# All paired groups of batches 2 and 3 through seven products that build on each other in PSUM

## The chip, the core and the metric

One core of a Trainium2 chip runs the whole program. The metric is the device time of one execution in microseconds (us), the median of some runs. The engines that matter here are TensorE (PE in the rows, its weight loads PEld), VectorE (DVE), ScalarE (ACT), GpSimd (POOL) and the queue of SyncE (SP), from which nearly all transfers are issued. TensorE's results go to eight banks of PSUM, which TensorE, VectorE and ScalarE reach.

## The reference

Capped attention, then two multi-layer parts with residuals, on 4 batches of 448 tokens and 768 columns:

```python
scores = cap * tanh(q @ k.T / sqrt(64) / cap)           # 12 heads of 64
attn = exp(scores - max) / (sum + 1e-9) @ v             # -> x: (4, 448, 768)
xn = (x - mean) / sqrt(var + 1e-6) * g_ln
x = x + relu(xn @ w_ch1) @ w_ch2                        # 768 -> 3072 -> 768
h = relu(x.T @ w_tok1) @ w_tok2                         # tokens: 448 -> 256 -> 448
u = x + h.T
y = u + relu(u @ w2_ch1) @ w2_ch2                       # 768 -> 1536 -> 768
```

## The kernel before

Activations lie transposed: `X[b][e]` is a block of 128 columns of batch `b` by 448 tokens, six blocks a batch. Every number that enters a product is kept as two halves, a rounded high one and the rest (`split`: ScalarE or VectorE copies the high half at L180 or L182, VectorE subtracts for the low half at L176), and a product takes three passes (`PASSES`), so it is three matmuls of 128x128 by 448 for each pair of blocks.

The channel layers are worked off in groups of 4 hidden blocks (512 hidden columns): 6 groups of the first MLP, 3 of the second. `mlp` runs a group directly, for one batch or two (first layer L926, second layer L899); a batch takes 144 matmuls a group, two take 288. For batches 2 and 3 most groups go another way: `strassen` treats the two batches and the halves of a weight block as a 2x2 problem and makes seven products where eight are direct, 252 matmuls (L713). For this it needs sums of quarter blocks of weights (`a11`, `a12`, `a21`, `a22` give `s1` to `s4`, in `sums`) and sums of the activations (`X1` to `X4`, in `sides`; `b11`, `b21` are batch 2's halves in `BIG[0]`, `b12`, `b22` batch 3's in `BIG[1]`). `first_quads` makes the hidden blocks of a group (two quads, `q` = 0, 1; each product nine matmuls), then sums of them (`H1` to `H4`, L640), and `second_quads` the outputs (each product three times, `r` = 0 to 2, six matmuls).

Before, each product has a bank of its own from a ring of eight; the sums of products are made outside PSUM: ScalarE copies a product (`out_copy`, L704), VectorE adds others to it (`plus`, L701) or adds two SBUF tiles (`both`, L640). `sums` makes weight sums in a chain: `start` loads a quarter from DRAM, `more` lets a transfer issued by GpSimd add another quarter onto it (L676), `negate` is ScalarE (L682), then `split`.

The weights come as 64-bit words that `piece` decodes on ScalarE and VectorE; the decoded whole and its halves are stored to DRAM (L340, L369), from where later uses load them (L353, and L733 and L797 for paired groups). This is done while batches 0 and 1 go through `mlp`. Groups 0 and 6 are lone for batches 2 and 3 (`N1 = 1`, `N2 = 1`): batch 2 runs group 0 after its norm, batch 3 runs it woven into the token mixing of batch 2 (`tokens`: transposes L960, first layer L984, second L1006), batch 2 runs group 6 woven into the mixing of batch 3, and batch 3 runs it after that.

The order is not that of the code. `Program.emit` collects all steps with keys (`prog.key`, a due time in the planner's us, less an `early`), and always takes the engine that can go first and on it the ready step with the smallest key, by its own table of costs (`FIXED`, `RATE`, `LATER`). The constants ahead of the program set the keys. On every engine and queue the steps are then worked off strictly in that order, so a step that waits holds up what stands behind it. Names with `late_` (`late_qk`, `late_vs`, `late_x0` and so on) are tiles that take over the space of attention's tiles; `late_bank` are the four banks that attention's scores had. `split0` to `split2` and `late_whole` are eight half tiles (`part_ring`) that hold weights for products.

## Time and profile before

| | us |
|---|---|
| median of 3 runs | 1364.21 (1359.86 to 1368.12) |
| the profiled execution | 1362.73 |
| its span, first to last instruction | 1361.0 |
| TensorE busy in it | 1317.1 (97%) |
| VectorE busy | 1160.7 (85%) |
| ScalarE busy | 766.7 (56%) |
| GpSimd busy | 236.6 (17%) |

Attention and the norms of batches 0 and 1 take the first 180 us; until about 780 us batches 0 and 1 go through their MLPs and mixings while attention of batches 2 and 3 runs beside them; the paired groups of the first MLP stand at 838 to 1112 us, the mixings of batches 2 and 3 at 1112 to 1244, the last two paired groups behind. A row of the profile that names two tiles, as in "bank<-big,split", writes the first from the others; buffer numbers are left out.

### The profile page before, as it was taken

To read this page: it belongs to the slowest core of one execution; us is meant where nothing else is said; L and a number is where in the kernel's file an instruction comes from. 1 tells how busy PE (TensorE), PEld (TensorE's weight loads), DVE (VectorE), ACT (ScalarE), POOL (GpSimd) and SP (SyncE) were. 2 spreads that over 40 slices of the span, in tenths; PEclk is the share of its full clock that TensorE was granted. 3 is DMA by queue.
4 is the path that set the end of the run, shared out by engine and by line. 5 is a ranking of instruction groups with operands and counts; after the bars stand their busy time and mean duration, and the time that the engine had idled before them with its cause. 6 is when DMAs were issued, how large, how long until landed. Compare 5 with 4: busy or idle time off the path is not lost. (4 is left out here: it accounts for less than half of the span.)

```text
span 1361.0 us, 18258 instructions
## 1 busy us (share of the span) xinstructions
PE 1317.1 (97%) x6234; PEld 1128.5 (83%) x6234; DVE 1160.7 (85%) x1999; ACT 766.7 (56%) x1227; POOL 236.6 (17%) x196
## 2 busy tenths in 40 slices
PE   8899999999999999999999999899999999999997
PEld 4334589999999899988899989788988889999786
DVE  5989799999999999999999874878888884476698
ACT  8996667675766756866765322634535442223442
POOL 2420000110101001200000030333323320011221
PEclk9999999999999999999999999999999999999899
DMA  7885357777777868466777587687787884357685
GB/s 279 307 276 194 119 185 250 276 256 284 247 253 263 281 236 279 151 222 224 246 249 246 199 258 246 133 189 168 172 188 166 199 212 143 116 170 184 133 196 129
DMA packets 163021, 290.12 MB, mean 213 GB/s; under 512 B 12016, under 2 KB 105840, under 8 KB 162928
## 3 DMA queue, kind: packets, MB, share of 16 engines
q1 hardware_dynamic: 131888, 266.64, 57.9%
q0 software_dynamic: 30464, 22.03, 11.9%
q8 instruction: 49, 0.80, 0.3%
q10 hardware_dynamic: 576, 0.29, 0.1%
q14 instruction: 44, 0.36, 0.1%
HBM read 203.39 MB, written 85.52 MB: 212 GB/s over the span
## 5 line engine op out<-in xcount | busy, mean ns | idle before, releaser
L899 PE MATMUL bank<-h,split 128*128 128x448 f32 x1452 | 312.4, 368 | 4.0 <-DMA split<-kept 1.8
L926 PE MATMUL bank<-big,split 128*128 128x448 f32 x1404 | 299.2, 368 | 0.5 <-DVE split L176 0.5
L899 PEld LDWEIGHTS bank<-h,split 128*128 128x128 f32 x1452 | 271.4, 188 | 29.2 <-issue 3.6
L926 PEld LDWEIGHTS bank<-big,split 128*128 128x128 f32 x1404 | 262.6, 188 | 25.2 <-issue 1.6
L176 POOL TENSOR_TENSOR ks<-qk,ks 64x512 fp32r<-64x512 f32 x24 | 34.6, 1444 | 497.1 <-ACT ks L419 488.3
L903 DVE TENSOR_TENSOR x<-x,bank 128x448 f32<-128x448 f32 x121 | 73.8, 610 | 24.3 <-PE bank L899 23.6
L180 ACT ACTIVATE split<-whole 128x512 fp32r<-128x512 f32 (+1 forms) x70 | 50.4, 721 | 60.5 <-PE bank L899 24.5
L931 ACT ACTIVATE h<-bank 128x448 fp32r<-128x448 f32 x78 | 42.1, 540 | 64.5 <-PE bank L926 64.3
L333 ACT ACTIVATE whole<-raw 128x512 f32<-128x512 f32 (+2 forms) x94 | 70.7, 752 | 12.5 <-DMA raw<-in_w 6.8
L336 DVE SCALAR_TENSOR_TENSOR whole<-raw,whole 128x512 int32<-128x512 int32 (+2 forms) x94 | 74.1, 788 | 0.1
L337 DVE CUSTOM_DVE_ANT_0 whole<-raw,whole 128x1024 uint16<-128x1024 uint16 (+2 forms) x84 | 71.3, 849 | 0.1
L334 ACT ACTIVATE raw<-raw 128x512 int32<-128x512 uint32 (+2 forms) x94 | 71.2, 758 | 0.1
L176 DVE TENSOR_TENSOR split<-whole,split 128x512 fp32r<-128x512 f32 (+1 forms) x80 | 64.9, 812 | 0.8 <-ACT split L180 0.6
L446 DVE TRANSPOSE_TENSOR_REDUCE m<-x 128x28 f32<-128x896 f32 x48 | 52.9, 1105 | 12.3 <-ACT x L442 11.9
L441 ACT ACTIVATE own<-sc,tsc 128x896 f32<-128x896 f32 x48 | 48.2, 1004 | 15.2 <-DVE x L502 7.9
L713 PE MATMUL bank<-big,split 128*128 128x448 f32 x222 | 52.7, 375 | 2.3 <-ACT split L180 2.2
L932 DVE SCALAR_TENSOR_TENSOR h<-bank,h 128x448 fp32r<-128x448 f32 x78 | 47.7, 611 | 8.1 <-ACT h L931 7.9
L335 DVE TENSOR_SCALAR whole<-whole 128x512 int32<-128x512 int32 (+2 forms) x94 | 52.3, 557 | 1.9 <-ACT whole L333 1.8
L446 DVE TRANSPOSE_TENSOR_REDUCE m<-own 128x28 f32<-128x896 f32 x48 | 52.7, 1097 | 0.9 <-ACT own L442 0.9
L493 DVE TRANSPOSE_TENSOR_REDUCE n<-own 128x28 f32<-128x896 f32 x48 | 52.5, 1097 | 0.0
L442 ACT ACTIVATE own<-own,cap_t 128x896 f32<-128x896 f32 x48 | 50.0, 1042 | 0.6
L438 PE MATMUL sc<-qs,ks 128*128 128x448 f32 x192 | 48.1, 371 | 1.9 <-ACT own L441 1.4
(426 smaller groups left out, 2803.1 us busy)
## 6 DMA issues: line engine op xcount, KB each, us to landing
split<-kept SPq DMA_DIRECT2D x94, 384.0 KB, 4.4
raw<-in_w SPq DMA_DIRECT2D x36, 768.0 KB, 5.4
kept<-split SPq DMA_DIRECT2D x36, 768.0 KB, 4.2
raw<-in_w SPq DMA_DIRECT2D x54, 512.0 KB, 3.8
split<-kept SPq DMA_DIRECT2D x42, 512.0 KB, 3.9
keeps<-split SPq DMA_DIRECT2D x42, 512.0 KB, 3.8
qk<-in_qkv SPq DMA_DIRECT2D x33, 480.0 KB, 4.3
whole<-whole SPq DMA_DIRECT2D x28, 384.0 KB, 2.8
```

What stands on the lines that cost most here:

```text
L176: eng.tensor_tensor(out, whole, high.bitcast(F32), op=ALU.subtract)
L333: add("act", m * 1.1, lambda: act(f.bitcast(F32), hi.bitcast(F32), AF.Copy, scale=2.0 ** -112), [r], [w])
L334: add("act", m * 1.1, lambda: act(lo, lo.bitcast(U32), AF.Copy, scale=2.0 ** -29), (), [r])
L335: add("dve+", m // 2, lambda: dve.tensor_scalar(f, f, 3, None, op0=ALU.logical_shift_left), (), [w])
L336: add("dve+", m, lambda: dve.scalar_tensor_tensor(f, hi, -(1 << 31), f, op0=ALU.bitwise_and, op1=ALU.bitwise_or), [r], [w])
L337: add("pool+" if ahead else "dve+", m, lambda e: engine_of[e].tensor_tensor(f, f, lo, op=ALU.add), [r], [w])
L446: add("dve", 2 * S, lambda half=half, e=e: dve.tensor_reduce(m.at[:, half].rearrange("p c j -> p (c j)"), e.rearrange("p c (j i) -> p (c j ...
L493: add("dve", 2 * S, lambda half=half, e=e: dve.tensor_reduce(n.at[:, half].rearrange("p c j -> p (c j)"), e.rearrange("p c (j i) -> p (c j ...
L713: mm(bank.at[:, :S], w(wi), x.at[:, xi], start=(i, n) == (0, 0), stop=(i, n) == (len(parts) - 1, 2))
L899: mm(py.at[:, :S], w[:, wi, i * P:(i + 1) * P], h[i].at[:, hi], start=(i, n) == (0, 0), stop=(i, n) == (G - 1, 2))
L903: add("dve", S, lambda x=x, py=py: dve.tensor_tensor(x.at, x.at, py.at[:, :S], op=ALU.add), [py], [x], early=EVACUATE)
L926: mm(ph.at[:, :S], w[:, wi, cc * P:(cc + 1) * P], src[cc].at[:, xi], start=(cc, n) == (0, 0), stop=(cc, n) == (NCC - 1, 2))
```

## The change

All nine groups of batches 2 and 3 are paired (`N1 = 0`, `N2 = 0`), and the mixings of the two batches are woven with each other (`tokens(2)` with `tokens(3)`). In a quad the product `a11*b11` stays in its bank: ScalarE copies it, and `s2*X2`, then `s1*X1`, then `s4*b22` are added onto it in the same bank by matmuls that don't start a new sum; `s3*X3` and `a22*X4` share another bank. `second_quads` does the same in three banks each, and VectorE adds each stage to `X`. Banks are handed out from a list (`spare`). Weight sums are made by four loads and four VectorE additions of 384 columns (`narrow`). `sides` takes the norm's results or `X` as they are where it can, and goes through its kinds one after another. In `tokens`, the second layer takes all three blocks with the first hidden block, then all three with the second. The wholes of second-layer weights are stored in another layout. All constants that set keys and some of the planner's costs are new.

The diff, cut to its core:

```diff
-URGENT, SCORES, PREPARE, LOAD = 1000.0, 19.31, 4.58, 24.58
+URGENT, SCORES, PREPARE, LOAD = 1000.0, 14.37295, 3.25093, 26.17876
...
-N0, N1, N30, N20, N2 = 1, 1, 0, 1, 1
...
+N0, N1, N30, N20, N2 = 1, 0, 0, 1, 0
...
+T_ATT2, PACE2, T_ATT3, PACE3 = 200.92224, 35.97238, 678.45284, 26.41417
...
-QUAD_LEAD, SUM_LEAD, SIDES_LATER, SIDES_PACE, X_LATER = 16.0, 24.0, 20.0, 4.0, 4.0
+QUAD_LEAD, SUM_LEAD, SIDES_LATER, SIDES_PACE, HIDDEN_LATER, FIRST = 3.35595, 16.17507, -13.10765, 1.12559, -1.8455, 0.95664
...
-            add("dma", m, lambda: nc.sync.dma_start(out=whole.at, in_=g), [w], [whole])
+            rows = g if m == C else g.rearrange("p (a d) -> p a d", a=G)
+            add("dma", m, lambda: nc.sync.dma_start(out=whole.at, in_=rows), [w], [whole])
...
-                    of_group[grp] = dp.tile([P, NCC, 2, cols], F32, name=f"keeps{grp}"), dp.tile([P, NCC, cols], F32, name=f"wholes{grp}")
+                    of_group[grp] = dp.tile([P, NCC, 2, cols], F32, name=f"keeps{grp}"), dp.tile([P, G, NCC, P], F32, name=f"wholes{grp}")
...
+    def sides(later, x2, x3, between=None):
+
+        t, t0 = [next(tmps) for _ in range(3)], prog.key
+        more = ring([next(tmps), next(tmps)])
+        for kind in range(4):
+            for c in range(3):
+                prog.key = t0 + later + (3 * kind + c) * SIDES_PACE
+                b12, b22, to = x3[c], x3[3 + c], t[c]
+                if kind == 0:
+                    b11 = x2[c] if x2 else to
+                    if not x2:
+                        join(b11, BIG[0][c], S)
+                    both(to, b12, b11, ALU.subtract, S)
+                elif kind == 1:
+                    both(to, to, b22, ALU.subtract, S)
+                elif kind == 2:
+                    to = next(more)
+                    both(to, b22, b12, ALU.subtract, S)
+                else:
+                    to = next(more)
+                    b21 = x2[3 + c] if x2 else to
+                    if not x2:
+                        join(b21, BIG[0][3 + c], S)
+                    both(to, b21, t[c], ALU.add, S)
+                split((X1, X2, X3, X4)[kind][c], to, S)
+            if kind == 2 and between:
+                between()
...
-    def sums(chunks, a11, a12, a21, a22, s1, s2, s3, s4):
...
-        def start(f, a):
-            at, boxes = a
...
-        def more(f, a):
-            at, boxes = a
-            add("pool", CC, lambda: nc.gpsimd.dma_start(out=shaped(f, at), in_=at, accum_op=ALU.add), boxes, [f], lag=4.0)
...
-        def negate(f):
-            add("act", CC, lambda: act(f.at, f.at, AF.Copy, scale=-1.0), (), [f])
...
-        split(s1, fa, CC)
-        negate(fa)
-        more(fa, a11)
-        split(s2, fa, CC)
-        more(fa, a12)
+    def sums(f11, f12, f21, f22, a11, a12, a21, a22, s1, s2, s3, s4):
+
+        def narrow(to, a, b, op):
+            add("dve+", CC, lambda: dve.tensor_tensor(to.at[:, :CC], a.at[:, :CC], b.at[:, :CC], op=op), [a, b], [to])
+
+        for f, (at, boxes) in ((f21, a21), (f22, a22), (f11, a11), (f12, a12)):
+            add("dma", CC, lambda f=f, at=at: nc.sync.dma_start(out=f.at[:, :CC], in_=at), boxes, [f])
+        narrow(f22, f21, f22, ALU.add)
+        narrow(f21, f11, f21, ALU.subtract)
+        narrow(f11, f11, f22, ALU.subtract)
+        split(s2, f11, CC)
+        split(s3, f21, CC)
+        narrow(f12, f12, f11, ALU.add)
...
-        split(s3, fb, CC)
+        split(s1, f22, CC)
         yield
-        split(s4, fa, CC)
+        split(s4, f12, CC)
...
+    def take():
+        return spare.pop(0)
+
+    def product(bank, parts, n_parts, first):
...
-                    mm(bank.at[:, :S], w(wi), x.at[:, xi], start=(i, n) == (0, 0), stop=(i, n) == (len(parts) - 1, 2))
+                    mm(bank.at[:, :S], w(wi), x.at[:, xi], start=first and (i, n) == (0, 0), stop=(i, n) == (len(parts) - 1, 2), skip_group_check=not first)
...
+    def quad(g, q):
...
+        a11, a12 = direct(row, 0), direct(row, CC)
+        c11 = next(tmps)
+        pa, pd = take(), take()
+        times(pa, a11, b11, first=True)
+        out_copy(c11, pa)
+        times(pd, a12, b21, first=True)
+        plus(c11, pd, c11)
+        spare.append(pd)
+        rectify(c11)
+        split(H11[q], c11, S)
+        yield
+        s2, s3, s1 = (next(part_ring) for _ in range(3))
+        a22, s4 = direct(row2, CC), next(part_ring)
+        prog.key -= SUM_LEAD
+        for _ in sums(*(next(wfs) for _ in range(4)), block(row, 0), block(row, CC), block(row2, 0), block(row2, CC), s1, s2, s3, s4):
+            pass
+        prog.key += SUM_LEAD
+        c21, c22, c12 = (next(tmps) for _ in range(3))
+        pc = take()
+        times(pa, s2, X2)
+        out_copy(c21, pa)
+        times(pc, s3, X3, first=True)
+        out_copy(c22, pc)
+        yield
+        times(pa, s1, X1)
+        plus(c22, pa, c22)
+        rectify(c22)
+        times(pc, a22, X4)
+        plus(c21, pc, c21)
+        spare.append(pc)
+        rectify(c21)
+        split(H21[q], c21, S)
+        split(H22[q], c22, S)
+        yield
+        times(pa, s4, b22)
+        rectify(c12, pa)
+        spare.append(pa)
+        prog.key += HIDDEN_LATER
+        both(c11, c12, c11, ALU.subtract, S)
+        both(c12, c22, c12, ALU.subtract, S)
+        both(c22, c11, c22, ALU.subtract, S)
+        both(c21, c21, c22, ALU.add, S)
+        split(H2[q], c22, S)
+        split(H3[q], c12, S)
+        split(H1[q], c11, S)
+        split(H4[q], c21, S)
+        prog.key -= HIDDEN_LATER
+        yield
...
+        def onto(b, e, bank):
+            plus(X[b][e], bank, X[b][e])
+
+        pa = [take() for _ in range(3)]
         for r in range(3):
-            p = times("a11", r, H11)
-            out_copy(t[r], p)
-            plus(X[2][r], p, X[2][r])
+            onto(2, r, times(pa, "a11", r, H11, first=True))
             yield
         further(QUAD_LEAD)
+        pd = [take() for _ in range(3)]
         for r in range(3):
-            p = times("a12", r, H21)
-            plus(X[2][r], p, X[2][r])
+            onto(2, r, times(pd, "a12", r, H21, first=True))
             final(2, r)
             yield
...
+        spare.extend(pd)
...
         for r in range(3):
-            plus(t[r], times("s2", r, H2), t[r])
-            both(w[r], w[r], t[r], ALU.add, S)
-            both(X[3][r], X[3][r], w[r], ALU.add, S, -X_LATER)
-            both(X[3][3 + r], X[3][3 + r], w[r], ALU.add, S, -X_LATER)
+            onto(2, 3 + r, times(pa, "s2", r, H2))
+            yield
+        further(QUAD_LEAD)
+        pc = [take() for _ in range(3)]
+        for r in range(3):
+            onto(3, 3 + r, times(pc, "s3", r, H3, first=True))
             yield
         for r in range(3):
-            p = times("s3", r, H3)
-            plus(X[3][3 + r], p, X[3][3 + r])
+            onto(3, 3 + r, times(pa, "s1", r, H1))
             final(3, 3 + r)
-            plus(t[r], p, t[r])
-            both(X[2][3 + r], X[2][3 + r], t[r], ALU.add, S, -X_LATER)
             yield
         for r in range(3):
-            plus(X[3][r], times("s4", r, H22), X[3][r])
+            onto(2, 3 + r, times(pc, "a22", r, H4))
+            final(2, 3 + r)
+            yield
+        spare.extend(pc)
+        for r in range(3):
+            onto(3, r, times(pa, "s4", r, H22))
             final(3, r)
             yield
-        for r in range(3):
-            plus(X[2][3 + r], times("a22", r, H4), X[2][3 + r])
-            final(2, 3 + r)
-            yield
+        spare.extend(pa)
...
         def second(half, hT):
-            for e in range(3 * half, 3 * half + 3):
-                pu, xb, g = next(main_banks), X[b][e], u[e]
-
-                def product(e=e, pu=pu):
-                    a = (e % 3) * P
-                    for j in range(2):
+            banks = {}
+            for j in range(2):
+                for e in range(3 * half, 3 * half + 3):
+                    if j == 0:
+                        banks[e] = next(main_banks)
+                    pu, xb, g = banks[e], X[b][e], u[e]
+
+                    def product(e=e, pu=pu, j=j):
...
+                    pe(3 * S, product, [hT[j], T2[j]], [pu])
+                    if j == 1:
...
+                    yield
...
-        relay()
-        sides(SIDES_LATER)
+        sides(SIDES_LATER, None, centred, relay())
...
+        spare += [next(main_banks) for _ in range(8)]
         weave(strassen(groups((2, 3), n1, NG1 - n1)))
+        main_banks = ring(list(spare))
...
-        weave(tokens(2, HIDDEN[2]), mlp(groups((3,), N30, n1 - N30)), ahead=TOKENS_AHEAD)
-        weave(tokens(3, HIDDEN[2]), mlp(groups((2,), NG1, n2)), ahead=TOKENS_AHEAD)
-        sides(SIDES_LATER)
+        if N30 < n1 or n2:
+            weave(tokens(2, HIDDEN[2]), mlp(groups((3,), N30, n1 - N30)), ahead=TOKENS_AHEAD)
+            weave(tokens(3, HIDDEN[2]), mlp(groups((2,), NG1, n2)), ahead=TOKENS_AHEAD)
+        else:
+            weave(tokens(2, HIDDEN[1]), tokens(3, HIDDEN[2]), ahead=TOKENS_AHEAD)
+        sides(SIDES_LATER, None if N2 else X[2], X[3])
...
+        spare[:] = [next(main_banks) for _ in range(8)]
         weave(strassen(groups((2, 3), NG1 + n2, NG2 - n2), True))
```

Three places show what the new order does. The first is TensorE's queue at the start of the first paired group, after the last direct group of batch 1 (second layer, `h`, `split`). Before, lone work of batch 2 (`big_80` is its normed input) stands there:

```order
L899 MATMUL bank_114<-h_85,split_75 128x448 x3
L926 MATMUL bank_112<-big_80,split_73 128x448 x18
L926 MATMUL bank_113<-big_80,split_74 128x448 x18
L926 MATMUL bank_114<-big_80,split_75 128x448 x18
L926 MATMUL bank_112<-big_80,split_73 128x448 x18
L899 MATMUL bank_113<-h_82,split_74 128x448 x3
```

Now the four opening products (`a11*b11`, `a12*b21` of both quads) follow, then `s3*X3` (`late_raw`), `s2*X2` (`late_x_6293`), `a22*X4` (`late_own`, `qs`) and `s1*X1` (`late_x_6037`):

```order
L923 MATMUL bank_114<-h_85,split_75 128x448 x3
L722 MATMUL late_bank_5364<-big_80,split_73 128x448 x9
L722 MATMUL bank_111<-big_80,split_73 128x448 x9
L722 MATMUL late_bank_5365<-big_80,split_74 128x448 x9
L722 MATMUL bank_112<-big_80,split_74 128x448 x9
L722 MATMUL late_bank_5366<-late_raw,split_75 128x448 x9
L722 MATMUL late_bank_5364<-late_x_6293,split_75 128x448 x9
L722 MATMUL late_bank_5366<-late_own,late_whole 128x448 x6
L722 MATMUL late_bank_5366<-qs_97,late_whole 128x448 x3
L722 MATMUL late_bank_5364<-late_x_6037,late_whole 128x448 x9
```

The 144 matmuls of the lone group are gone, and products that build on each other come back to `late_bank_5364` and `late_bank_5366` with one product between them.

The second is TensorE's queue in the token mixings. Before, the mixing of batch 2 (second layer with `t_70`, first layer with `t_69`, transposes with `kc`) stands between matmuls of the lone group of batch 3 (L899):

```order
L899 MATMUL late_bank_5496<-h_84,split_73 128x448 x3
L899 MATMUL late_bank_5496<-h_85,split_73 128x448 x3
L899 MATMUL late_bank_5493<-h_82,split_74 128x448 x3
L899 MATMUL late_bank_5493<-h_83,split_74 128x448 x3
L984 MATMUL late_bank_5496<-big_80,t_69 128x384 x6
L984 MATMUL late_bank_5496<-h_88,t_69 128x384 x3
L984 MATMUL late_bank_5496<-h_89,t_69 128x384 x2
L899 MATMUL late_bank_5493<-h_84,split_74 128x448 x3
L899 MATMUL late_bank_5493<-h_85,split_74 128x448 x3
L960 MATMUL bank_112<-kc,x_79 128x128 x3
```

Now steps of batch 2 (`x_78`, `big_80`, and `h_82`, `h_83`) and batch 3 (`x_79`, `big_81`) stand between each other:

```order
L984 MATMUL bank_114<-kc,other_96 128x128 x3
L1008 MATMUL bank_112<-big_80,t_69 128x384 x5
L1008 MATMUL bank_111<-big_81,t_69 128x384 x6
L984 MATMUL late_bank_5364<-kc,x_78 128x128 x3
L984 MATMUL late_bank_5367<-kc,x_78 128x128 x3
L1008 MATMUL bank_111<-big_81,t_69 128x384 x5
L984 MATMUL late_bank_5366<-kc,x_78 128x128 x3
L984 MATMUL bank_112<-kc,other_96 128x128 x3
L1008 MATMUL late_bank_5365<-big_81,t_69 128x384 x6
L1033 MATMUL late_bank_5364<-t_70,h_82 128x448 x3
L1033 MATMUL late_bank_5367<-t_70,h_82 128x448 x3
```

Only the other batch's mixing is left between two steps of one batch.

The third is the weight sums of group 1 (`whole_5` and `wholes_158` are its stored wholes). Before, they stand on GpSimd's queue, each an adding transfer:

```order
L676 DMA late_pair<-wholes_158 128x3x128
L676 DMA late_qk<-wholes_158 128x3x128
L676 DMA late_vs<-whole_5_152 128x384
L676 DMA v<-wholes_158 128x3x128
L676 DMA late_vs<-whole_5_152 128x384
L676 DMA v<-wholes_158 128x3x128
```

Now GpSimd has no transfers, and VectorE's queue has, between an addition from PSUM (L709) and low halves (L180), the additions at L692:

```order
L692 TENSOR_TENSOR mean_109<-late_qk,mean_109 128x384
L692 TENSOR_TENSOR late_qk<-late_pair,late_qk 128x384
L692 TENSOR_TENSOR late_pair<-late_pair,mean_109 128x384
L709 TENSOR_TENSOR late_qk<-late_bank_5367,late_qk 128x448
L692 TENSOR_TENSOR other_96<-late_vs,other_96 128x384
L180 TENSOR_TENSOR late_whole<-late_pair,late_whole 128x384
L692 TENSOR_TENSOR late_vs<-v,late_vs 128x384
L180 TENSOR_TENSOR late_two<-late_qk,late_two 128x448
L692 TENSOR_TENSOR v<-v,other_96 128x384
```

The sums have moved from GpSimd's and ScalarE's queues into VectorE's, among the additions that free PSUM.

## Rows read from the trace of the kernel before

**Rows 1.** The page's first part: busy us, share of the span, instructions.

```profile
PE 1317.1 (97%) x6234; PEld 1128.5 (83%) x6234; DVE 1160.7 (85%) x1999; ACT 766.7 (56%) x1227; POOL 236.6 (17%) x196
```

**Rows 2.** Stretches: length, busy us of each engine, granted clock, DMA share, GB/s.

```profile
180.00:780.00 600.00, 596.55 (x2959) 545.44 (x2958) 581.30 (x969) 397.97 (x602) 62.77 (x44) 1.00 0.70 243
...
838.00:900.00 62.00, 56.77 (x265) 50.40 (x264) 42.49 (x80) 26.10 (x53) 17.97 (x17) 0.97 0.73 160
900.00:1112.00 212.00, 206.30 (x998) 186.25 (x997) 184.95 (x353) 102.91 (x198) 67.71 (x62) 1.00 0.83 182
1112.00:1244.00 132.00, 131.00 (x673) 120.12 (x672) 74.70 (x125) 34.49 (x67) 13.09 (x11) 1.00 0.50 156
1244.00:1361.00 117.00, 105.65 (x490) 93.69 (x488) 91.87 (x172) 48.96 (x95) 28.13 (x26) 0.95 0.69 158
```

**Rows 3.** Waits of TensorE, 838 to 1361 us: total us, times, longest.

```profile
PE bank L713 <- ACT split L180: 4.6, 3, 2.2
PE late_bank L713 <- ACT split L180: 2.8, 2, 1.9
PE late_bank L713 <- DVE split L176: 1.8, 2, 1.3
PE bank L713 <- DVE late_whole L176: 1.6, 1, 1.6
PE late_bank L713 <- DVE split L182: 1.2, 1, 1.2
```

**Rows 4.** TensorE in order of time, two group starts: start, us, operation, count.

```profile
954.72 1.99 PE L713 MATMUL late_bank<-big,split 128*128 128x448 f32 x9
956.55 1.99 PE L713 MATMUL bank<-big,split 128*128 128x448 f32 x9
...
1008.46 2.02 PE L713 MATMUL bank<-big,split 128*128 128x448 f32 x9
1010.32 2.02 PE L713 MATMUL late_bank<-big,split 128*128 128x448 f32 x9
```

**Rows 5.** TensorE in order of time, first paired group; in brackets the hole before.

```profile
867.13 2.98 PE L713 MATMUL bank<-big,split 128*128 128x448 f32 x9 [2.22 <-ACT split L180]
869.91 2.44 PE L713 MATMUL late_bank<-big,late_whole 128*128 128x448 f32 x6
...
873.45 1.38 PE L713 MATMUL late_bank<-big,late_whole 128*128 128x448 f32 x6
```

**Rows 6.** VectorE in order of time, a later paired group; in brackets the idle time before.

```profile
957.93 0.61 DVE L701 TENSOR_TENSOR x<-bank,x 128x448 f32<-128x448 f32 x1
958.47 0.61 DVE L701 TENSOR_TENSOR x<-late_bank,x 128x448 f32<-128x448 f32 x1
...
963.09 0.56 DVE L176 TENSOR_TENSOR late_whole<-v,late_whole 128x384 fp32r<-128x384 f32 x1 [3.01 <-ACT late_whole L180]
963.56 0.62 DVE L701 TENSOR_TENSOR rstd<-bank,mean 128x448 f32<-128x448 f32 x1
```

**Rows 7.** Transfers: queue, count, KB each, median us from issue to landing.

```profile
v<-whole POOLq DMA_DIRECT2D x21, 192.0 KB, 4.6
...
late_pair<-whole SPq DMA_DIRECT2D x7, 192.0 KB, 3.8
```

**Rows 8.** ScalarE, two groups from 954.72: busy us, mean ns, idle before, releaser.

```profile
L180 ACT ACTIVATE late_whole<-v 128x384 fp32r<-128x384 f32 x4 | 2.1, 525 | 6.2 <-DMA v<-whole 5.4 <-PE bank L713 0.8
...
L704 ACT ACTIVATE sq<-bank 128x448 f32<-128x448 f32 x2 | 1.1, 527 | 0.0
```

**Rows 9.** TensorE in order of time, token mixings: start, us, operation, count.

```profile
1125.67 0.82 PE L960 MATMUL bank<-kc,x 128*128 128x128 f32 x6
1126.24 1.46 PE L926 MATMUL late_bank<-big,split 128*128 128x448 f32 x6
...
1156.98 1.23 PE L984 MATMUL late_bank<-big,t 128*128 128x384 f32 x6
1158.05 1.03 PE L984 MATMUL late_bank<-h,t 128*128 128x384 f32 x5
```

174 lines of the change are left out of this document (58 added, 116 removed).

## The prediction

> **What bounds the kernel now.** I read the page's first part first, then busy time by stretches, then the waits of TensorE, then TensorE and VectorE in order of time. TensorE is busy 1317.1 of 1361.0 us [rows 1]: the end is set by the number of matmuls and by the holes between them. The stretches show where the holes are [rows 2]: 3.5 us between 180 and 780 us, 5.2 in 838 to 900 (the first paired group), 5.7 in 900 to 1112 (four more), 1.0 in 1112 to 1244 (both token mixings, with lone groups woven in), 11.4 in 1244 to 1361 (the last two paired groups and the last output). What ends the holes after 838 us is in the waits [rows 3]: 4.6 + 2.8 + 1.8 + 1.6 + 1.2 = 12.0 us for the halves of a weight block or weight sum, almost nothing for PSUM. One such case is seen on VectorE: it stands for 3.01 us [rows 6] until ScalarE has split `v`, and ScalarE stood 5.4 us in four such places for the transfer that adds to `v` [rows 8]. Some holes cost twice, because the clock falls behind them: after a hole of 2.22 us nine matmuls take 2.98 us and six take 2.44, where nine take 1.99 [rows 4] and six 1.38 at full clock, so 2.05 us [rows 5]; the granted clock is 0.97 in 838 to 900 and 0.95 in 1244 to 1361 [rows 2], one such stretch of half clock (1.2 GHz) in the first and, besides the end of the program, two in the second.
>
> A matmul of 448 columns is worth 1.83 / 9 = 0.203 us at one time and 1.86 / 9 = 0.207 us at another, both at full clock [rows 4]. A paired group has 7 x 36 = 252 of them, 51.2 to 52.1 us; the one that starts at 954.72 takes 53.74 us [rows 4], so 1.6 to 2.5 us of a group are holes.
>
> **The change part by part.** The sum starts from the profiled execution, 1362.7 us (span 1361.0 and 1.7 around it); the median of the runs is 1364.2.
>
> *Fewer matmuls.* Two more groups go through seven products in place of eight: 2 x (288 - 252) = 72 matmuls of 448 columns go, and the order lists them so, 6001 matmuls before and 5929 now. TensorE is the bound there: 72 x 0.203 to 0.207 = **-14.7 us**. Up to the last norm of batch 3 the order is nearly the same (3139 matmuls of 448 columns ahead of it before, 3151 now), so the first 780 us move by no more than the 3.5 us of holes in 180 to 780, either way; I take 0.
>
> *Weight sums.* Before, a set of four sums is a chain: load, adding transfer on GpSimd's queue, ScalarE's negation, the next adding transfer; the adding ones land 4.6 us after issue [rows 7]. Now four plain loads, which depend on nothing but their buffers, land after about 3.8 us [rows 7] and four additions on VectorE make all sums. VectorE pays for them: an instruction of 128x448 starts 0.54 us after the one before it, one of 128x384 0.47 us [rows 6]. A group had 69 of the first (35 additions from PSUM, 20 in SBUF, 14 low halves) and 16 of the second: 37.3 + 7.5 = 44.8 us. It now has 49 (27, 8 and 14) and 32: 26.5 + 15.0 = 41.5 us. So VectorE gets lighter by 3 us a group although it takes the sums over, because products that build on each other in PSUM spare 20 additions; it has some 10 us of a group's 51.7 to spare. The 56 negations and 112 adding transfers leave the program. Of the 12.0 us of waits for weights I keep 0.4 us a group, 3.6 for nine: **-8.4 us**. Bounds: all gone, -12.0; as much per group as before, 12.0 x 9 / 7 = 15.4, +3.4. I stand nearer to the first since the chain that made them is gone, but the additions queue in order on VectorE.
>
> *Half clock.* If the holes shrink, so do the falls behind them. I keep one of three stretches of 2.05 us: **-4.1 us** (bounds 0 and -6.2).
>
> *Products upon each other.* A product that is added to a bank must wait until the bank has been read. In a quad the copy of the bank (0.53 us on ScalarE [rows 8]) or the addition from it (0.61 us [rows 6]) runs beside one product of nine matmuls on another bank, 1.83 us [rows 4]; in the second layer three such banks rotate, so the slack there is larger. I take 0, and the case that it isn't hidden is a rival below. The Trainium skill ("PSUM — Partial Sum Buffer", PSUM bank collisions raise a hardware error) has TensorE and a reader kept apart by whole banks, so the wait can't be avoided by reading other columns; it speaks against this part, and no run so far shows its price here.
>
> *Filler that goes.* Ahead of the first paired group, lone work of batch 2 no longer covers the norm of batch 3 and the side sums. Counted in the new order, TensorE has 48 + 72 matmuls of the last group of batch 1 and 36 opening products (which need only batch 2 and plain weights) between the norm's last matmul and the first product that needs a side sum: 156 x 0.205 = 32 us. VectorE has 34 instructions there until that side sum is whole, at most 34 x 0.54 = 18 us, and 53 until the next product's, 29 us. So it is covered, with some 4 us of slack. At the second side sums, TensorE has 42 matmuls (8.6 us) from the product that ends batch 3's fourth block of columns to the first product with a side sum of that block, and VectorE 10 instructions (5.4 us) until the sum's first part, 14 (7.6 us) until its last: covered by 1 to 3 us. The token mixings now cover only each other: 88 matmuls of 384 columns at 1.07 / 6 = 0.18 us, 72 of 448 at 0.205 and 48 transposes at 0.57 / 6 = 0.095 [rows 9], 35 us of TensorE; VectorE has 24 instructions of 384 and 24 of 448 there, 24 us. Each link (product, ScalarE's copy, VectorE's rest, next product) is some 1.3 us, and the other batch has 1 to 4 us of work for it. I charge **+2.5 us** for links that show (bounds 0 and, if each of the three places shows 3.3 us, +10).
>
> *With one answer:* the side sums take the two operands of the norm or of X as they lie, and 18 joins go (they lay beside TensorE's work); the whole weights are now stored in pieces of 512 bytes, 54 stores in place of 42, beside a mid-part whose TensorE has no holes; ScalarE, busy 103 of 212 us [rows 2], loses negations and copies. All 0.
>
> Sum: 1362.7 - 14.7 - 8.4 - 4.1 + 2.5 = **1338.0 us**.
>
> **The rivals.** *A, the new waits take the place of the old.* If the addition that frees a bank for the third product in a quad stands behind three other VectorE instructions, it ends 3 x 0.54 + 0.61 + some 0.2 = 2.4 us after its product, 0.6 us too late; at 18 quads that is 11 us, and the time is 1338 + 11 = 1349. For it: VectorE is over 80% busy and works in order. Against: before, no wait of the kind is among the long ones [rows 3], though there a bank came round only after eight products. Chance 0.15.
>
> *B, VectorE stands for the weights, slower than before.* The four loads of a set can be issued only when the set before has let go of its buffers, and the additions wait for them at the head of VectorE's queue; behind them stand the additions that free PSUM. VectorE has some 10 us of a group to spare, 2.5 us for each of four sets. If every one of the 36 sets costs the full landing of 3.8 us, TensorE loses 36 x 1.3 = 47 us: 1338 + 47 = 1385. From 2.5 + 33 / 36 = 3.4 us a set it is over 1371. For it: the 3.01 us for a late weight now [rows 6]. Against: the loads are asked for ahead and don't depend on each other. Chance 0.07; lesser stalls of this kind, which end within 0.5% of now, 0.08.
>
> *C, all holes go.* With no waits for weights, no half clock and no link that shows the sum is 1362.7 - 14.7 - 12.0 - 6.2 = 1330, and with the 3.5 us of the first part and all nine groups at 0.203 (4 us) some 1322. Chance 0.10 for less than 1327.
>
> *D, the gate.* Where filler goes, a hole may grow until the clock falls, as after 2.22 us [rows 5]. The Trainium skill ("TensorE: Matmul & The Clock Gate", Part 1) says that a TensorE that idles drops to half its clock and needs work to get it back; the row agrees. Each new stretch costs 2.05 us; three more, at the norm, the mixings and the second side sums, would give 1338 + 6 + their holes, some 10, so 1354. It is within A's class and I give it 0.05 of its own.
>
> **How the numbers follow.** The forecast, 1327 to 1348, has 0.55; A 0.15, C 0.10, D 0.05: together 0.85 faster than the median by more than 0.5% (below 1357.4), which is about what a measurement of this kernel can tell from no change. 0.08 lie within 0.5%, 0.07 are slower (over 1371.0). The range takes in the bounds: up to the half of what lies above D, down to C's 1322. All bad bounds at once give 1362.7 - 14.7 + 3.4 + 10 = 1361; I stop at 1357. That the change doesn't do what it says is excluded by the order for the matmuls.
>
> **What would show it.** Right: a paired group takes 52 to 53 us, waits of TensorE for weight halves sum to under 5 us after 780 us, GpSimd is idle there, the two token mixings take under 40 us, and at most one stretch of half clock is left before the end. Wrong: waits of the product's line on additions from PSUM (A), VectorE idle behind loads of whole weights (B), holes at the norm or side sums with half clock behind them (D). If the mid-part before 780 us moves by more than 4 us, the step on the order was wrong.

## The result

The changed kernel takes 1321.24 us (median of 4 runs, 1318.34 to 1328.15) where the kernel before took 1365.12 beside it (1359.86 to 1368.12): a ratio of 0.969, 95% interval 0.9642 to 0.9738. The profiled execution took 1321.3 us, span 1319.5, so 41.4 us less than the 1362.7 from which the sum started. The forecast was 1338, 17 us above the measured time. The number is that of the third rival, "all holes go" (1322), but its mechanism did not come: 7.0 us of waits for weights and one stretch of half clock are left, the paired groups two to five still step at 0.207 us in this profile, and parts that nothing had priced gave time back. The direction was right, and so was the count of matmuls; the size of the holes that would go was not.

The page's first line for the changed kernel, against [rows 1]:

```profile
PE 1293.1 (98%) x6162; PEld 1115.3 (85%) x6162; DVE 1180.4 (89%) x2085; ACT 769.1 (58%) x1229; POOL 103.7 (8%) x74
```

TensorE has 72 executions fewer (6234 to 6162) and is busy all but 26.4 us; it was idle for 43.9. The stretches, against [rows 2] (length, busy us of PE, its weight loads, DVE, ACT and POOL, granted clock, DMA share, GB/s); they are cut at the first paired product, the first group's end, the token mixings, and the end of the first group behind them:

```profile
805.00:862.00 57.00, 53.45 (x253) 48.44 (x253) 46.92 (x91) 23.48 (x44) 0.00 (x0) 0.97 0.48 150
862.00:1120.00 258.00, 258.00 (x1251) 234.27 (x1250) 215.13 (x412) 109.08 (x210) 0.00 (x0) 1.00 0.50 153
1120.00:1158.00 38.00, 37.75 (x221) 35.79 (x220) 30.08 (x58) 18.88 (x41) 0.00 (x0) 1.00 0.09 27
1158.00:1213.50 55.50, 52.08 (x254) 47.37 (x254) 53.27 (x104) 27.62 (x53) 0.00 (x0) 1.00 0.41 128
1213.50:1319.50 106.00, 102.32 (x505) 94.49 (x504) 84.54 (x160) 42.04 (x81) 0.00 (x0) 1.00 0.48 151
```

From 862 to 1120 us TensorE is not idle once: 258.00 of 258.00 us. What is left after 805 us stands in three places: the two groups that open a stretch of paired work (3.6 and 3.4 us of idle time), and behind the last matmul. The waits of TensorE from 779 us to the end, against [rows 3] (total us, times, longest), say the same:

```profile
PE bank L722 <- ACT split L184: 5.7, 2, 3.2
PE bank L923 <- DMA split<-keeps: 0.9, 1, 0.9
PE bank L722 <- DVE split L180: 0.8, 2, 0.4
PE bank L722 <- DMA split<-keeps: 0.5, 1, 0.5
PE late_bank L1014 <- DVE h L1017: 0.2, 1, 0.2
```

**Where 41.4 us went.** I took the time from each 448-column matmul's start to the next and summed what exceeds 0.2025 us, apart for matmuls that were stretched by a hole or half clock (0.215 us and more) and for the rest:

| part | before | after | us |
|---|---|---|---|
| 72 matmuls at 0.2025 | | | -14.6 |
| first 160 us (8 matmuls fewer done by then) | | | +1.6 |
| stretched, 160 us to the norm of batch 3 | 12.3 | 9.0 | -3.3 |
| stretched, norm to first paired group | 3.8 | 1.1 | -2.7 |
| stretched, the two opening groups | 16.7 | 9.9 | -6.8 |
| stretched, the other paired groups (5, then 7) | 10.2 | 0.0 | -10.2 |
| stretched, mixings and what is woven in | 2.8 | 0.6 | -2.2 |
| step of the unstretched matmuls | 8.9 | 8.0 | -0.9 |
| last matmul's end to the span's end | 6.6 | 3.8 | -2.8 |
| not assigned | | | +0.5 |

### The profile page after: what moved, and what is told of

Read it like the earlier page. It is cut to its first block, busy times and chain, and to the rows that moved or that the text cites. A ratio compares the mean times of both kernels' runs of the same rounds, so it can differ in the third digit from the quotient of the medians.

```text
span 1319.5 us, 18050 instructions
## 1 busy us (share of the span) xinstructions
PE 1293.1 (98%) x6162; PEld 1115.3 (85%) x6162; DVE 1180.4 (89%) x2085; ACT 769.1 (58%) x1229; POOL 103.7 (8%) x74
## 4 chain that ended last, share of the span: by engine, by line
PE 79%; DVE 11%; ACT 5%; DMA 2%; issue 2%; POOL 0%; SPq 0%; ACTq 0%; DVEq 0%
PE late_bank L722 19%; PE bank L923 18%; PE bank L950 17%; PE bank L722 14%; PE sc L450 2%; PE bank L468 2%; PE bank L492 2%; ACT x L453 1%; DVE m L458 1%; ACT x L454 1%; DMA raw<-in_w 1%; PE bank L1008 1%; PE bank L1033 1%; DVE n L505 1%; DVE el L180 1%
## 5 line engine op out<-in xcount | busy, mean ns | idle before, releaser
L923 PE MATMUL bank<-h,split 128*128 128x448 f32 x1296 | 276.0, 367 | 1.3 <-DMA split<-keeps 0.9
L950 PE MATMUL bank<-big,split 128*128 128x448 f32 x1296 | 275.8, 367 | 0.0
L923 PEld LDWEIGHTS bank<-h,split 128*128 128x128 f32 x1296 | 242.5, 188 | 22.8 <-DVE x L927 1.2
L950 PEld LDWEIGHTS bank<-big,split 128*128 128x128 f32 x1296 | 242.7, 188 | 21.7 <-issue 2.2
L722 PE MATMUL late_bank<-big,split 128*128 128x448 f32 x378 | 84.5, 367 | 0.0
L722 PEld LDWEIGHTS late_bank<-big,split 128*128 128x128 f32 x378 | 70.9, 188 | 6.6
L955 ACT ACTIVATE h<-bank 128x448 fp32r<-128x448 f32 x72 | 38.8, 540 | 61.2 <-PE bank L950 61.0
L709 DVE TENSOR_TENSOR x<-bank,x 128x448 f32<-128x448 f32 x107 | 65.4, 629 | 9.3 <-PE bank L722 8.2
L180 POOL TENSOR_TENSOR ks<-qk,ks 64x512 fp32r<-64x512 f32 x24 | 34.2, 1424 | 494.5 <-ACT ks L431 460.3
L927 DVE TENSOR_TENSOR x<-x,bank 128x448 f32<-128x448 f32 x108 | 65.9, 611 | 3.7 <-PE bank L923 2.9
L180 DVE TENSOR_TENSOR split<-whole,split 128x512 fp32r<-128x512 f32 (+1 forms) x80 | 65.3, 817 | 0.3
L722 PE MATMUL bank<-h,split 128*128 128x448 f32 x240 | 56.0, 373 | 6.5 <-ACT split L184 5.7
L458 DVE TRANSPOSE_TENSOR_REDUCE m<-x 128x28 f32<-128x896 f32 x48 | 52.9, 1105 | 10.2 <-ACT x L454 9.7
L722 PEld LDWEIGHTS bank<-h,split 128*128 128x128 f32 x240 | 45.5, 191 | 12.0 <-ACT split L184 6.5
L709 DVE TENSOR_TENSOR x<-late_bank,x 128x448 f32<-128x448 f32 x82 | 50.2, 629 | 6.0 <-PE late_bank L722 5.6
```

The costliest lines, as they stand in the source:

```text
L180: eng.tensor_tensor(out, whole, high.bitcast(F32), op=ALU.subtract)
L458: add("dve", 2 * S, lambda half=half, e=e: dve.tensor_reduce(m.at[:, half].rearrange("p c j -> p (c j)"), e.rearrange("p c (j i) -> p (c j ...
L709: add("dve", S, lambda: dve.tensor_tensor(to.at, bank.at[:, :S], t.at, op=ALU.add), [bank, t], [to], early=FIRST)
L722: mm(bank.at[:, :S], w(wi), x.at[:, xi], start=first and (i, n) == (0, 0), stop=(i, n) == (len(parts) - 1, 2), skip_group_check=not first)
L923: mm(py.at[:, :S], w[:, wi, i * P:(i + 1) * P], h[i].at[:, hi], start=(i, n) == (0, 0), stop=(i, n) == (G - 1, 2))
L927: add("dve", S, lambda x=x, py=py: dve.tensor_tensor(x.at, x.at, py.at[:, :S], op=ALU.add), [py], [x], early=EVACUATE)
```

## Experiments: which part took the holes

Four kernels undo one part each. All times of this section are to be held against 1321.2 (changed) and 1363.2 (before, beside these four).

**The lone groups back.**

```diff
-N0, N1, N30, N20, N2 = 1, 0, 0, 1, 0
+N0, N1, N30, N20, N2 = 1, 1, 0, 1, 1
```

> The changed kernel with one lone group of each layer-half for batches 2 and 3 again (all else as changed). Theory: the pairing is worth its matmuls and no more; 72 matmuls of 448 columns come back, 72 x 0.205 = +14.8 us, while lone work again covers the two openings of paired work, which hold 3.6 and 2.9 us of waits and one half-clock stretch of 2 us, so up to 8.5 us is given back: 1327 to 1336 us. Rival: lone work in between brings holes of its own (the before kernel's share of the missing 17 us): over 1340 us. VectorE and the weight sums are as in the changed kernel, so the paired groups in mid-stretch should still run without any hole.

1343.58 us (1339.44 to 1346.04), ratio to before 0.984 (0.980 to 0.987). The paired groups in mid-stretch run without a hole, as expected (52.08 us each, four in a row), but lone work gave nothing back at the openings. Waits of TensorE:

```profile
PE late_bank L722 <- ACT split L184: 6.0, 1, 6.0
PE bank L722 <- ACT split L184: 3.1, 1, 3.1
PE bank L923 <- DVE late_raw L180: 3.1, 1, 3.1
```

The first opening shows the same 3.1 us at the same product as the changed kernel, and the second 6.0 where that has 2.55. So 14.6 us of the 22 are the matmuls. Of the rest, the two openings have 14.7 us of stretched matmuls where the changed kernel has 9.9, and 5.2 in place of 1.1 stand ahead of the first one, in the direct groups (the third wait above). Lone work doesn't cover the openings: what delays TensorE there is not a lack of other work.

**The weight sums by adding transfers again.**

```diff
+        start(f22, a21)
+        start(f21, a21)
+        more(f22, a22)
+        negative(f21, f21)
+        more(f21, a11)
+        negative(f11, f22)
+        more(f11, a11)
         split(s2, f11, CC)
+        more(f11, a12)
...
-QUAD_LEAD, SUM_LEAD, ... = 3.35595, 16.17507, ...
+QUAD_LEAD, SUM_LEAD, ... = 3.35595, 24.0, ...
```

The edit also takes the `narrow` additions out and sets the planner's cost of a transfer back to the older form.

> The changed kernel with the weight sums made as before: load, adding transfer on GpSimd's queue, negation on ScalarE, adding transfer (lead of the sums 24 as before). Products still build on each other in PSUM, so VectorE is lighter than in either kernel (some 34 us of a group's 52). Theory: the chain of transfers made the holes; 1.3 us of waits for weight halves a group come back, 9 x 1.3 = 12 us, with 2 to 6 us of half clock behind them: 1333 to 1340 us, waits of TensorE for weight halves over 10 us after 780 us. Rival: the holes went because VectorE has slack now, not because of the chain: within 3 us of 1321, waits under 6 us.

1352.67 us (1348.59 to 1357.04), 31 us above the changed kernel and more than the theory gave. Each paired group in mid-stretch has its hole again: 53.3 to 56.4 us. VectorE, the third number of busy time in this row, is busy for only 35.5 of 53 us there, so its slack alone doesn't take the holes away:

```profile
913.00:966.00 53.00, 52.06 (x254) 47.36 (x253) 35.52 (x67) 24.71 (x48) 14.01 (x16) 1.00 0.77 178
```

But the waits are not where I had put them; TensorE's, and the largest of GpSimd's queue (which waits for the negations on ScalarE):

```profile
PE late_bank L734 <- DMA split<-kept: 10.1, 2, 5.2
PE bank L734 <- DMA split<-keeps: 9.8, 5, 3.2
PE bank L734 <- DVE split L179: 2.1, 3, 0.9
```

```profile
POOL v L699 <- ACT v L702: 141.2, 18, 31.7
```

It is the plain weight halves that come late. With the lead of before for these (16 us in place of 3.4):

> The weight sums on GpSimd's queue again as in the run before, and the plain weight halves asked for 16 us ahead as the kernel before had it, where the run before asked for them 3.4 us ahead. In that run 22 us of waits were for plain halves that landed late, because they stood behind loads of whole weights that waited for the chains' buffers. Theory: with the older lead those waits go and what is left is the chains' own price: 1333 to 1340 us. Rival: the queue is held up whatever the lead, since the chains hold the buffers: over 1345 us.

1355.93 us (1352.66 to 1357.21): no better, and the same waits (10.9 and 8.0 us). So the lead is not it. The holder that I named, a load of a whole weight at the head of SP's queue, is there in the second group of each stretch. The half that TensorE waited for until 899.07 us (3.15 us) was issued right behind such a load, which had stood for 4.4 us until the adding transfer into its buffer had landed:

```profile
SPq L695 <- DMA late_vs<-wholes: 4.4, 1, 4.4
```

```profile
893.31 0.32 SPq L695 DMA_DIRECT2D late_vs<-whole  x1
893.68 0.43 SPq L833 DMA_DIRECT2D split<-keeps  x1
```

The wait of 3.62 us at the same place of the second stretch has the same rows before it. The two longest waits, in the opening groups, have another holder. At the first (5.08 us, ended at 848.77 us) the half was asked for at 843.12, and what SP waited for until then was TensorE, which still read the half's own buffer:

```profile
SPq L760 <- PE bank L734: 2.6, 1, 2.6
```

That the chains bring holes into every group in mid-stretch is shown, and in the second groups the way is through SP's queue. Why the two longest waits come stays open; at this place TensorE goes to the next group's quad with four of the seven products of the second layer still to come, so the planner's order may have a part in it.

**The seven products of a quad in banks of their own.**

```diff
-        times(pa, s2, X2)
-        out_copy(c21, pa)
+        plus(c21, alone(s2, X2), c11)
+        plus(c11, p2, c11)
...
+        plus(c12, alone(s1, X1), c21)
+        plus(c22, p7, c12)
+        plus(c21, p7, c21)
```

> The changed kernel with the seven products of each first-layer quad in a bank of their own again, summed on VectorE by 7 additions where the changed kernel has 3; the second layer and the weight sums stay as changed. VectorE pays 8 x 0.54 = 4.3 us more a group: 41.5 + 4.3 = 45.8 us of 51.2 to 52.2, about what it had before (44.8). Theory (the chain of transfers made the holes, VectorE's load did not): still within 5 us of 1321. Rival: VectorE's slack took the holes away; then 1 to 2.5 us a group come back, 1330 to 1344 us, as waits of TensorE for splits.

1345.06 us (1342.42 to 1346.42). My theory falls here: VectorE is busy for 46.2 of 52 us, and in this order that is already too much:

```profile
966.00:1018.00 52.00, 50.85 (x248) 45.89 (x247) 46.16 (x90) 19.53 (x36) 0.00 (x0) 1.00 0.50 152
```

Groups in mid-stretch take 53.2 to 53.6 us, 2.1 of it stretched; the two openings lose 22 us. Waits of TensorE:

```profile
PE bank L722 <- DVE late_two L180: 10.0, 2, 5.2
PE bank L722 <- ACT h L184: 4.2, 6, 0.7
PE bank L722 <- DVE h L180: 1.9, 6, 0.3
```

They are for the hidden activations (`late_two`, `h`). At the first opening ScalarE has written the high half of `late_two` and VectorE comes to the low half 5.8 us later, behind eleven other instructions, in a row from 831.6 us on without a break (rows below). The edit adds load and moves steps at once, and the planner's numbers are those of the changed kernel; whether another order of the same load would be free of holes was not run.

```profile
835.07 0.58 ACT L184 ACTIVATE late_two<-sum 128x448 fp32r<-128x448 f32 x1
```

```profile
841.43 0.62 DVE L180 TENSOR_TENSOR late_two<-sum,late_two 128x448 fp32r<-128x448 f32 x1
```

**The planner's numbers of before.**

```diff
-URGENT, SCORES, PREPARE, LOAD = 1000.0, 14.37295, 3.25093, 26.17876
+URGENT, SCORES, PREPARE, LOAD = 1000.0, 19.31, 4.58, 24.58
...
-QUAD_LEAD, SUM_LEAD, SIDES_LATER, SIDES_PACE, HIDDEN_LATER, FIRST = 3.35595, 16.17507, -13.10765, 1.12559, -1.8455, 0.95664
+QUAD_LEAD, SUM_LEAD, SIDES_LATER, SIDES_PACE, HIDDEN_LATER, FIRST = 16.0, 24.0, 20.0, 4.0, 0.0, 0.0
```

> The changed kernel with the planner's numbers of before (leads, paces, costs; the two new ones at 0), nothing else. Theory: the structure carries the gain and the numbers little; the first 780 us give back their 3.6 us, the paired part up to 5 more: 1322 to 1330 us. Rival: the missing 17 us are the order's, set by the numbers: 1335 us or more, with waits for weight halves or side sums back in the paired groups.

1349.49 us (1348.42 to 1353.41): the rival held. 27.0 us of stretched matmuls are in the two opening groups (9.9 in the changed kernel), 1.3 to 1.4 in five others, and the first paired product starts 7.5 us later (812.3 against 804.8). So the structure without its numbers is worth 14 us of the 44.

The four prices (22, 31, 24, 28 us) are together far more than the gain: the holes that come back stand at different places, and none of the four kernels has planner's numbers made for it. The prices say which holes come back, not what share of the gain a part has.

## Experiments: what is left at the openings

**Without the opening, and with the mixings apart.**

```diff
-            yield from first_quads(g, g == plan[0][0])
+            yield from first_quads(g, False)
```

> The changed kernel without the opening: the first quads of a stretch run one after the other, so the 36 products that need no side sum don't stand ahead; 18 of them (3.7 us) come later. By the prediction's own count (32 us of TensorE against 29 us of VectorE with the opening) the side sums then show by some 1 us at the first stretch, and at the second (8.6 us against 5.4 to 7.6) by 0 to 3 us; with the first-order buffers as in later groups the holes at the weight sums (3.5 and 3.4 us, half clock 2 us) may go: 1314 to 1325 us. Rival: the side sums are far behind, and each opening shows 4 us or more and a half-clock stretch: 1329 us or more.

1321.70 us (1318.10 to 1323.26), no difference: 9.7 us of stretched matmuls at the two openings against 9.9. But they are others: the long waits at the weight sums are gone, and shorter ones (1.6 us for a hidden half, 1.2 for a plain weight half, 1.1 for an addition, and less) have come. None of these is a wait for a side sum.

```diff
-            weave(tokens(2, HIDDEN[1]), tokens(3, HIDDEN[2]), ahead=TOKENS_AHEAD)
+            weave(tokens(2, HIDDEN[1]), ahead=TOKENS_AHEAD)
+            weave(tokens(3, HIDDEN[2]), ahead=TOKENS_AHEAD)
```

> The changed kernel with the token mixings of batches 2 and 3 one after the other, without lone work beside them. Theory: each of some 10 links of a mixing (product, copy, low half, next product) shows its 1.3 us less the work of its own batch that stands ready, so 5 to 13 us for the two, with one or two half-clock stretches: 1327 to 1338 us; the mixings take 45 us or more in place of 38. Rival: a mixing covers itself, since its products of the other half stand ready: within 3 us of 1321.

1328.40 us (1324.84 to 1330.53), inside what I expected, but by another mechanism. From the first transpose to the last product of the mixings there are 40.8 us, of which nine matmuls of the next paired group are 1.9, where the changed kernel has 38.4: a mixing all but covers itself, as the rival said. The loss is in the paired group behind (12.1 us of stretched matmuls where the changed kernel has 4.2), at the first product with a weight sum (start, us, operation, the hole before it):

```profile
1196.13 0.74 PE L722 MATMUL bank<-h,split 128*128 128x448 f32 x1 [5.86 <-ACT split L184]
```

**One buffer.** Why that product, in the changed kernel and in those with lone groups, old numbers and mixings apart? The changed kernel's rows at the first opening, TensorE, then SP's queue, then VectorE, then ScalarE:

```profile
837.06 0.77 PE L722 MATMUL late_bank<-late_two,split 128*128 128x448 f32 x3
841.00 0.47 PE L722 MATMUL bank<-h,split 128*128 128x448 f32 x1 [3.17 <-ACT split L184]
841.86 2.23 PE L722 MATMUL bank<-h,split 128*128 128x448 f32 x5 [0.38 <-DVE split L180]
```

```profile
834.10 0.32 SPq L695 DMA_DIRECT2D rstd<-wholes  x1
```

```profile
838.90 0.55 DVE L692 TENSOR_TENSOR rstd<-late_vs,rstd 128x384 f32<-128x384 f32 x1
...
839.84 0.56 DVE L692 TENSOR_TENSOR late_vs<-v,late_vs 128x384 f32<-128x384 f32 x1
...
840.77 0.56 DVE L692 TENSOR_TENSOR v<-v,rstd 128x384 f32<-128x384 f32 x1
```

```profile
840.43 0.52 ACT L184 ACTIVATE split<-late_vs 128x384 fp32r<-128x384 f32 x1 [0.41 <-DVE late_vs L692]
```

The weight sums of the second layer borrow four of the quads' buffers. In a group that opens a stretch, both quads take their `c11` first, so the ring hands the second quad's `c11`, which comes free last, to the sum that the others of its set need first (`rstd`, `f22`). Its load is issued at 834.10, its addition runs at 838.90 and the split that TensorE waits for at 840.43. The load itself landed 2.3 us after its issue, at 836.4; until 838.90 VectorE had other instructions ahead of the addition, without a break. So the late buffer acts through the order, in which the additions of this set stand far back, and not as a stand at the load. The same place of the second stretch has a hole of 2.55 us:

```profile
1194.53 0.47 PE L722 MATMUL bank<-h,split 128*128 128x448 f32 x1 [2.55 <-ACT split L184]
```

A few lines hand the four out in turned order in such a group:

```diff
-        f22, f12 = ([next(tmps) for _ in range(2)] for _ in range(2))
+        four = [next(tmps) for _ in range(4)]
+        if opening:
+            four = four[1:] + four[:1]
+        f22, f12 = four[:2], four[2:]
```

> The changed kernel with one edit in the second layer of the group that opens a stretch of paired work: the four buffers that its weight sums borrow are handed out in turned order, so that the one which the opening quad frees last (its c11) holds the fourth sum, needed last, and not the first. Theory: the two holes that are left (3.17 + 0.38 us at the first product with a weight sum in the first group, 0.50 + 2.55 + 0.38 us at the same place of the first group after the token mixings, and one half-clock stretch of 2 us behind the first) come from the load of a whole weight that waits for that buffer: 5 to 8.5 us go, 1313 to 1316 us. Rival: VectorE is behind with the hidden sums there, whatever the buffers: within 2 us of 1321.

1315.43 us (1311.35 to 1318.87), ratio to before 0.963 (0.961 to 0.966). The kernel without the opening fits this: it loses the late buffer and what the opening's products cover at once, some 6 us either way by the medians; that reading is argued from the two runs, not shown by a third. The late buffer is now the fourth sum, in place of 3.17 and 0.38 us there are holes of 0.15, 0.38 and 0.85, and the clock doesn't fall:

```profile
837.91 0.47 PE L722 MATMUL late_bank<-h,split 128*128 128x448 f32 x1 [0.15 <-ACT split L184]
838.77 1.09 PE L722 MATMUL late_bank<-h,split 128*128 128x448 f32 x4 [0.38 <-DVE split L180]
840.71 0.47 PE L722 MATMUL late_bank<-h,split 128*128 128x448 f32 x1 [0.85 <-DVE h L180]
```

Both once more, on one chip, with the old numbers and the turned order as a third:

> The changed kernel itself, with no edit, beside the two below on one chip. 1321 us as its median. It is run for a second profile of the same instruction stream: in the first, a matmul of 448 columns took 0.207 us from 845 to 1118 us without a hole, while the kernel with the mixings apart, whose stream on TensorE is the same up to the mixings, took 0.2025 there (52.1 and 51.1 us a group). Theory: the step has two values which the code doesn't set, so this profile may show either, and a paired group without holes takes 52.1 or 51.1 us. Rival: the stream sets it; then 52.1 again in groups two to five.

> The kernel with the turned order of the borrowed buffers again, beside the changed kernel on one chip: 5 to 7 us below it by the median (1314 to 1316 if that is at 1321), with holes at the weight sums of the opening groups under 3.2 us each.

> The planner's numbers of before together with the turned order of the borrowed buffers. With those numbers alone the two opening groups had 12.1 and 14.9 us of stretched matmuls, at the same place as in the changed kernel (the load into the buffer rstd was issued at 848.4 us, after the product that it delayed had been reached). Theory: the buffers' order made most of it whatever the numbers: 8 to 18 us go, 1331 to 1341 us. Rival: the old numbers put VectorE behind there, and the buffer is second: over 1345 us.

The changed kernel took 1320.36 us (ratio 0.9663, 0.9640 to 0.9687), the turned one 1312.65 (0.9609, 0.9585 to 0.9633): 7.7 us less, a little more than expected, and the best kernel here. In the profiles of these two, the openings have 11.5 and 5.4 us of stretched matmuls, so 6.1 us of it are there. The old numbers with the turned order took 1337.64 (1335.91 to 1338.26), 12 us less than without it: stretched matmuls at the openings fall from 27.0 to 15.4 us. (In the run without it the delayed load was issued at 848.4, some 1.6 us before TensorE came to the product, not after, as I had written.) The turned order is worth 7.7 us with the new numbers and 12 with the old, so the new numbers hide some 4 us of what the buffer costs. The numbers themselves are a matter apart: with the buffer turned in both, the old ones are still 25 us slower (1337.64 against 1312.65), so the buffer explains only some 3 of the 28 us that they cost in the changed kernel.

## Why the prediction was right and wrong

*Fewer matmuls, -14.7:* right. 72 executions are gone; at the step of the changed kernel that is 14.6 us. That the first 780 us stand still to within 3.5 us held at its edge: the last matmul of batch 3's norm ends at 779.0 in place of 780.1 with 12 matmuls more ahead of it, so 3.5 us went; stretched matmuls fell by 3.3.

*Weight sums, -8.4:* wrong as a size, twice. I kept 0.4 us for each of nine groups because VectorE works in order. Seven groups have no wait at all, and the two openings have 7.0 us between them, for a reason (the buffer) that the order of the code could have told. So the waits that this term counted fell from 12.0 to 7.0 us, by 5.0 and not 8.4. And [rows 3] held only the long waits for weight halves: with the half clock that the sum had apart (6.2) they make 18.2 us, where the paired groups had 26.9 us of stretched matmuls. The rest, 8.7 us, was short waits and their aftermath, which no term counted. Stretched matmuls went down by 17.0 us in the paired groups; the two terms, weight sums and half clock, had 12.5.

*VectorE lighter, 41.5 us a group:* right in size (215.13 us of busy time and 412 instructions in 258 us are 43.4 and 83 a group; I had 41.5 and 81), but it was priced at nothing as long as it fitted. With 46, which fit too, 2.1 us a group came back, since the hidden sums and low halves that TensorE waits for stand behind others in VectorE's order. Putting 8 of the 20 spared additions back cost 24 us in all, and the chain 31; neither is a share of the gain.

*Half clock, -4.1:* right in this profile; one fall is left, behind the hole of 3.17 us. The granted clock was 0.99 from 838 to 842 us, where TensorE was idle but for two matmuls, and 0.59 over the next four, most of them at the lower of its two levels (1.2 GHz):

```profile
838.00:842.00 4.00, 0.62 (x2) 0.33 (x2) 4.00 (x10) 1.71 (x4) 0.00 (x0) 0.99 0.59 197
842.00:846.00 4.00, 4.00 (x13) 3.59 (x14) 3.44 (x8) 0.00 (x0) 0.00 (x0) 0.59 0.61 197
```

This is the rule of the Trainium skill ("TensorE: Matmul & The Clock Gate", Part 1) that idling brings half the clock, and the rows agree. It was not the same in each execution: at the second opening the clock stayed at 1.00 behind the hole of 2.55 us, while in the second profile of the changed kernel the hole there was 3.14 us and the clock fell again, so that two falls were left:

```profile
1192.00:1196.00 4.00, 4.00 (x14) 3.59 (x13) 3.66 (x8) 0.00 (x0) 0.00 (x0) 0.57 0.78 225
```

*Products upon each other, 0:* right. No wait of a product for the reader of its bank is among the changed kernel's waits, so rival A did not come. The Trainium skill ("PSUM — Partial Sum Buffer", PSUM bank collisions raise a hardware error) has the engines kept apart by banks; the price of that here is nothing measurable. In a quad nine matmuls on another bank, 1.82 us, stand between two products on one bank, and the reading of a bank takes 0.53 to 0.62 us.

*Filler that goes, +2.5:* the step that failed most, with the wrong sign. I charged the loss of cover and looked for no gain. The stretched matmuls fell by 4.9 us instead: from 2.8 to 0.6 in the mixings, and from 3.8 to 1.1 in the passage from the norm to the first paired group, 7.4 us away from the term. The mixings take 38 us (under 40, as said), and cover themselves. At the second side sums the 4.2 us of stretched matmuls stand at the weight sum, not at a side sum. Rival D's holes at the openings came, though not from missing filler.

*Not in the sum:* 2.8 us behind the last matmul. Before, VectorE still had six additions to do then, two of them in SBUF; now one addition from PSUM is left. The first of the six, then the one:

```profile
1354.61 0.61 DVE L640 TENSOR_TENSOR x<-x,mean 128x448 f32<-128x448 f32 x1
```

```profile
1315.86 0.62 DVE L709 TENSOR_TENSOR x<-bank,x 128x448 f32<-128x448 f32 x1 [0.58 <-PE bank L722]
```

[Rows 2] had this in its last stretch, and I named it and didn't price it.

The 17 us between forecast and result are then: filler 7.4, paired groups 4.5 (17.0 in place of 12.5), the first part 3.3 (which I had taken at 0, with this much as its bound), the end 2.8, the step of the unstretched matmuls 0.9; against these stand 1.6 us in the first 160 us and 0.5 not assigned. So no part alone made the miss, and that the time came out at the third rival's number is luck in the main: of what that rival took away, only the first part went as it said (3.3 us, it had 3.5).

*Rival B* came in small and in another form: in the openings the weight sums are late because a load waits for a buffer, and TensorE stands 3.2 and 2.6 us; but VectorE doesn't stand for that load, it is busy with other instructions. Of what would show the forecast right, one item failed: waits for weight halves are 7.0 us in the paired groups, not under 5. A second, at most one stretch of half clock, held in the first profile and not in the second.

## What to carry over

When holes are spread over many instructions, count them from start-to-start times over the whole stretch; a list of the longest waits held less than half of the stretched time here. Whether an engine "fits" is told by its last instruction ahead of the one that waits, not by its busy share: in one order 46 busy us of 52 brought holes, in another 43 brought none. And where buffers go round in a ring, see which one comes free last and who gets it: turning four of them was worth 7.7 us, and the planner's numbers had hidden only some 4 us of what the buffer cost.

## What the hardware showed

A 448-column matmul at full clock takes 0.2025 or 0.207 us, and the code doesn't set which. The changed kernel's two profiles have the same stream on TensorE and the same hole at 838 us; in the first, the paired groups two to five take 52.08 us each, in the second 51.07. The same place in both, between holes (the second profile's last):

```profile
930.70 2.02 PE L722 MATMUL late_bank<-late_x,split 128*128 128x448 f32 x9
932.55 2.02 PE L722 MATMUL bank<-late_raw,split 128*128 128x448 f32 x9
```

```profile
930.21 1.99 PE L723 MATMUL late_bank<-late_x,split 128*128 128x448 f32 x9
932.03 1.99 PE L723 MATMUL bank<-late_raw,split 128*128 128x448 f32 x9
```

Starts are 1.85 us apart in one and 1.82 in the other, at a granted clock of 1.00 both times. Over the stretch from 862 to 1120 us that is 5 us, as much as several of the terms above, so single profiles of two kernels can differ by it. The step also changes within an execution. In the first profile it was the short one ahead of the hole at 838 us (here 1.82 us from start to start), the long one behind the half clock that followed, up to the token mixings, and the short one again in the last two groups (51.07 us each):

```profile
821.23 1.99 PE L722 MATMUL late_bank<-big,split 128*128 128x448 f32 x9
823.05 1.99 PE L722 MATMUL bank<-late_raw,split 128*128 128x448 f32 x9
```

In the second profile the like hole and half clock changed nothing, so they alone don't switch it. What does stays open; it wasn't tried.
